# Filling TensorE's planned waits in the opening with products of constants in any free PSUM bank (chunk-selected attention and a squared-ReLU layer, one core)

## The chip, the cores and the metric

The kernel runs on one core of one Trainium2 chip. TensorE (PE; its weight loads PEld) multiplies into PSUM, VectorE (DVE) and ScalarE (ACT) read PSUM and compute, GpSimd (POOL) computes and issues loads, SyncE (SP) issues stores and transposing DMAs. Times are device microseconds of one execution; the metric is the median over executions. The granted clock is the share of TensorE's full clock that was passed to it.

## The reference, cut to what matters

Inputs are q, k, v of 4 batches, 8 heads, 768 tokens, 64 dims, and two weights of 512 x 2048 and 2048 x 512, all f32.

```python
k_min, k_max = min and max of k over chunks of 32 tokens      # 24 chunks
ub     = sum_d maximum(q * k_min, q * k_max)                  # an upper bound of the scores per chunk
ub     = where(causal by chunk, ub, -1e9)
top    = the 6 chunks of largest ub, for each query
scores = where(chunk in top and causal, q k^T / 8, -1e9)
attn   = exp(scores - max) / (sum + 1e-9)
x      = (attn @ v), heads side by side                       # 3072 x 512
out    = relu(x @ w_in)^2 @ w_out                             # 3072 x 512
```

## The kernel before, in words

Tokens go in tiles of 128, six to a batch. In the first tile of a batch no chunk has to be chosen (a query sees at most 4), so the four first tiles have a path of their own. They are loaded with two tokens to a partition: batches 0 and 1 of k and q by SP as f32 (`raw`, L427), then converted to bf16 by DVE or ACT; batches 2 and 3 by GpSimd. `first_transposes` (L582) turns them with 16 transposes of 64 x 64 for each of k and q of a batch. `first_attention` then presets two PSUM banks with a causal mask (`preset`, L614: two products of 512 columns), adds the scores (L623, eight products), exponentiates on ACT (L639), multiplies with v (L630) and divides on DVE (`normalise`, L652 and L654). `turn_back` (L298, the helper `transpose`) brings the first keys back to token order (`kb`).

All other tiles go through pairs of heads. `stage_a` prepares one pair: transposes of keys and queries (`kT`, `qT`, L298), minimum and maximum of each chunk (`kr`, L753, DVE), the positive and negative parts of the queries (`qp`, `qm`, L769, DVE), bounds (`ub`, L703 and L705), the six best (`ubm` L778, `m` L711, `selb` L783, all DVE), the selection turned (`sT`) and copied beside the keys and queries (`kqc`, L292 on DVE, L290 on ACT). `stage_b` computes scores with the selection folded in (L839), exponentials (L861), causal masks (L816 and L819) and products with v (L850). `ffn` turns x (`xt`), multiplies by `w_in` (`up`, L923), applies ReLU and the square (L930, L932, L942), and multiplies by `w_out` (`down`, L955).

The order of all this is fixed ahead by a planner, the class `Plan`. Each operation has a due time, costs on the engines that may run it, the operations that it needs and the tiles that it uses. `order` keeps a time for each engine and for each PSUM bank (`tp` has 1, `ps` 3, `av` 2, `ff` 2), and picks what can start first; `write` then emits the operations in that order. Semaphore waits are put in from the data. The planner counts a TensorE operation double while its start lies before `WARM` (8.0 planned us).

The planner also fills TensorE's waits with work whose result nobody reads, so that TensorE isn't idle: the constant tile `warm` (all ones) is multiplied. This happens in two places. The operation `made["warm"]` opens TensorE's queue with 5 products of 512 columns. And in `order`, an operation that starts before `FILL` (26.0 planned us) and whose PSUM tiles are all new gets `fill` products, as many of 0.216 as fit in the time between TensorE's last operation, or the bank's release, and its start; they go into that operation's own new bank just ahead of it. Where the tile is bf16, four transposes of `warm` stand for each product. What comes of this rule in the program: four transposes of 128 x 128 ahead of batch 0's key transposes (`T`), and two products of 512 columns ahead of batch 3's presets.

Of the kernel before, what the change touches and what calls it, by code (L numbers as in the profile page):

```python
# [9 lines left out]
F32 = mybir.dt.float32  # L10
# [23 lines left out]
class Op:  # L34
    def __init__(self, where, due, fn, needs, tiles, packets, turns):
        self.where, self.due, self.fn, self.turns = where, due, fn, turns
        self.needs, self.tiles, self.packets = needs, tiles, packets
        self.engine = None
        self.start = self.end = None
        self.fill = 0  # L40


class Transfers:
# [37 lines left out]
class Plan:  # L81
# [8 lines left out]
    BUSY = 0.11  # L90
    SLOWER = {}
    WARM = 8.0
    FILL = 26.0
    NEVER = 1e9

    def __init__(self, slots, keep_warm, wait):
        self.wait = wait
        self.slots = slots
        self.keep_warm = keep_warm
        self.ops = []  # L100
        self.loads = []

# [14 lines left out]
    def order(self):  # L117
        free = {e: 0.7 for e in ("PE", "ACT", "DVE", "POOL", "SP")}
        slots = {tag: [(0.0, i) for i in range(n)] for tag, n in self.slots.items()}
        waiting = {}  # L120
        count = {}
        for op in self.ops:
            for t in op.tiles:
                t.left = len(t.users)
            count[op] = len(op.needs)
            for n in op.needs:
                waiting.setdefault(n, []).append(op)
        ready = [op for op in self.ops if not count[op]]
        landed, done = [], []
        port = {"DVE": 0.0, "POOL": 0.0}  # L130
        dma = Transfers()
        while ready:
            found = []
            for op in ready:
                if op.packets and not op.turns and op is not self.loads[len(landed)]:
                    continue
                at = 0.0
                new = {}
                for t in op.tiles:
                    if not t.held:  # L140
                        new[t.tag] = new.get(t.tag, 0) + 1
                for tag, n in new.items():
                    at = max(at, sorted(slots[tag])[n - 1][0]
                             if n <= len(slots[tag]) else self.NEVER)
                if at == self.NEVER:
                    continue
                if op.packets and not op.turns and len(landed) >= 8:
                    at = max(at, landed[-8].end)
                for engine, cost in op.where.items():
                    st = max(at, free[engine])  # L150
                    for n in op.needs:
                        same = n.engine == engine and not n.packets
                        lag = (0.0 if engine == "PE" else self.BUSY) if same                             else self.HAND_OVER[n.engine]
                        st = max(st, n.end + lag)
                    for t in op.tiles:
                        if t.psum:
                            for e, end in t.last.items():
                                if e != engine and "PE" not in (e, engine):
                                    st = max(st, end + self.HAND_OVER[e])
                    if op.port and engine in port:  # L160
                        st = max(st, port["DVE" if engine == "POOL" else "POOL"])
                    found.append((st, op, engine, cost))
            assert found, "nothing can start"
            first = min(found, key=lambda f: (f[0], f[1].number))
            st, op, engine, cost = min(
                (f for f in found if f[2] == first[2] and f[0] <= first[0] + self.wait),
                key=lambda f: (round(f[1].due, 6), f[0], f[1].number))
            ready.remove(op)
            if engine == "PE":
                op.fill = 0  # L170
                fresh = [t for t in op.tiles if t.psum]
                if st < self.FILL and fresh and not any(t.held for t in fresh):
                    room = max([free[engine]] + [min(slots[t.tag])[0] for t in fresh])
                    op.fill = max(0, int((st - room - 0.3) / 0.216))
                if st < self.WARM:
                    cost *= 2
            op.engine, op.start, op.end = engine, st, st + cost
            free[engine] = op.end
            if op.port and engine in port:
                port[engine] = op.end  # L180
            if op.packets:
                dma.add(op)
                if not op.turns:
                    landed.append(op)
            for t in op.tiles:
                if not t.held:
                    t.held = True
                    slot = min(slots[t.tag])
                    slots[t.tag].remove(slot)
                    t.slot = slot[1]  # L190
                t.last[engine] = max(t.last.get(engine, 0.0), op.end)
                t.left -= 1
                if not t.left:
                    slots[t.tag].append(
                        (max(u.end + self.HAND_OVER[u.engine] for u in t.users),
                         t.slot))
            for n in waiting.get(op, ()):
                count[n] -= 1
                if not count[n]:
                    ready.append(n)  # L200
            done.append(op)
        assert len(done) == len(self.ops), "operations left"
        return sorted(done, key=lambda op: op.start)

    def write(self):
        for op in self.order():
            for t in op.tiles:
                if t.tile is None:
                    t.tile = t.make(t.slot)
            if op.fill:  # L210
                self.keep_warm([t for t in op.tiles if t.psum][0].tile, op.fill)
            op.fn(op.engine)


# [1 line left out]
def kernel(  # L216
# [9 lines left out]
    nc = tc.nc  # L226
# [44 lines left out]
    psav = ctx.enter_context(tc.tile_pool(name="psav", bufs=1, space=PSUM))  # L271
# [3 lines left out]
    plan = Plan({"tp": 1, "ps": 3, "av": 2, "ff": 2, "e": 6, "h2": NFI + 6, "ht": 3,  # L275
                 "ob": 3, "kt": 3, "nt": 6,
                 "vn": B - 1, "x": 2, "xT": 2,
                 "st": 2, "kr": 2, "qp": 2, "qm": 2, "ubm": 2, "m8": 2, "rc": 2}, lambda *a: keep_warm(*a), P["wait"])
    POOLS = {"tp": pst, "ps": pss, "av": psav, "ff": psf, "e": epool, "h2": hpool,
             "ht": hpool, "ob": opool, "vn": ld, "nt": ldt, "kt": tpool}  # L280
# [16 lines left out]
    def transpose(dst, src):  # L297
        nc.tensor.matmul(dst, lhsT=src, rhs=ident, is_transpose=True,  # L298
                         start=True, stop=True)
# [5 lines left out]
    warm = consts.tile([128, 128], BF16, tag="warm")  # L305
# [55 lines left out]
    made = {}  # L361
# [176 lines left out]
    t_first = {}  # L538
    x_done = {}

    def keep_warm(dst, n):

        size = 1
        for dim in dst.shape[1:]:
            size *= dim
        dst = dst if len(dst.shape) == 2 else dst.rearrange(
            {3: "p a b -> p (a b)", 4: "p a b c -> p (a b c)"}[len(dst.shape)])
        if dst.dtype == F32:
            size = min(size, 512) // 128 * 128 or size
            for _ in range(n * 512 // size):  # L550
                nc.tensor.matmul(
                    dst[:, 0:size].rearrange("p (a b) -> p a b", b=min(size, 128)),
                    lhsT=warm, rhs=warm[:, 0:min(size, 128)].unsqueeze(1).to_broadcast(
                        [128, size // min(size, 128), min(size, 128)]),
                    start=True, stop=True)
        else:
            for _ in range(4 * n):
                transpose(dst[:, 0:128], warm)

    def warm_up(n):  # L560
        keep_warm(psav.tile([128, 4, 128], F32, tag="av.0", name="wt"), n)

    made["warm"] = plan.op({"PE": 1.08}, -999, lambda _: warm_up(5), [made["ones"]])

    class Turned:
        def __init__(self, b):
# [416 lines left out]
    for what in P["later"].split():  # L983
        nm, b = what[0], int(what[1])
        at = 20 * NP * b - 70 + 5 * "kqv".index(nm)
# [21 lines left out]
    for b in range(B):  # L1007
        x = buffer("x", [128, NS, d_model])
        x_done[b, 1] = []
        for p in range(NP * b, NP * (b + 1)):  # L1010
# [4 lines left out]
            x, lambda t, b=b: x_done[b, 1], [S * b + 128 * t for t in range(1, NT)],  # L1015
# [48 lines left out]
```

## Time and profile before

| what | us |
|---|---|
| median of 3 executions | 266.44 (265.9 to 266.63) |
| the profiled execution | 266.1 |
| its span, first to last instruction | 264.4 |
| TensorE busy in it | 253.8 |
| VectorE, ScalarE, GpSimd busy | 175.2, 187.0, 128.9 |
| mean granted clock of TensorE | 0.981 |

The rows below come from that one execution. In the rows of a timeline the first number is the start and the second the time from the first start to the last end of the group; `[1.92 <-X]` is idle time of the engine ahead of it, and what ended it. Products are pipelined on TensorE: the duration of one has a tail that lies beside the next.

### The profile page before, as it was taken

To read this page: it belongs to the slowest core of one execution; us is meant where nothing else is said; L and a number is where in the kernel's file an instruction comes from. 1 tells how busy PE (TensorE), PEld (TensorE's weight loads), DVE (VectorE), ACT (ScalarE), POOL (GpSimd) and SP (SyncE) were. 2 spreads that over 40 slices of the span, in tenths; PEclk is the share of its full clock that TensorE was granted. 3 is DMA by queue.
4 is the path that set the end of the run, shared out by engine and by line. 5 is a ranking of instruction groups with operands and counts; after the bars stand their busy time and mean duration, and the time that the engine had idled before them with its cause. 6 is when DMAs were issued, how large, how long until landed. Compare 5 with 4: busy or idle time off the path is not lost.

```text
span 264.4 us, 6715 instructions
## 1 busy us (share of the span) xinstructions
PE 253.8 (96%) x2479; PEld 164.4 (62%) x2479; DVE 175.2 (66%) x637; ACT 187.0 (71%) x377; POOL 128.9 (49%) x197
## 2 busy tenths in 40 slices
PE   6498999999999999999999999999999999999995
PEld 2375855666587666666678654667876544765443
DVE  6479999988799986986676993567876400455000
ACT  6278978879579997989978972789896511677111
POOL 8897789699769999996210770112111100000000
PEclk9659999999999999999999999999999999999999
DMA  7999999999993995999999921443010052100122
GB/s 125 170 182 162 175 142 182 169 131 178 184 144 75 130 160 127 78 165 158 154 136 159 198 47 59 119 93 98 2 40 2 10 131 92 69 0 2 40 79 79
DMA packets 112960, 29.40 MB, mean 111 GB/s; under 512 B 103328, under 2 KB 109984, under 8 KB 112928
## 3 DMA queue, kind: packets, MB, share of 16 engines
q0 software_dynamic: 73040, 13.11, 64.3%
q1 hardware_dynamic: 39888, 15.87, 29.3%
q8 instruction: 19, 0.31, 0.5%
q14 instruction: 13, 0.11, 0.1%
HBM read 27.26 MB, written 6.29 MB: 127 GB/s over the span
## 4 chain that ended last, share of the span: by engine, by line
PE 80%; DMA 6%; DVE 5%; ACT 4%; issue 2%; SPq 1%; ACTq 0%; DVEq 0%
PE py L955 29%; PE ph L923 28%; PE ps L839 12%; PE av L850 6%; DMA sT<-selb 4%; DMA raw<-in_q_dram 3%; ACT e L861 2%; DVE kqc L292 1%; PE kT L298 1%; ACT ht L930 1%; PE T L582 1%; PE qT L298 1%; SPq L427 1%; DVE m L711 1%; PE ps L623 1%
## 5 line engine op out<-in xcount | busy, mean ns | idle before, releaser
L923 PE MATMUL ph<-xT,w_in_sb 128*128 128x256 bf16 (+2 forms) x592 | 95.6, 304 | 0.3 <-ACT ht L930 0.2
L955 PE MATMUL py<-w_out_sb,h 128*128 128x512 bf16 (+2 forms) x400 | 90.5, 370 | 0.0
L861 ACT ACTIVATE e<-ps 128x512 bf16<-128x512 f32 x160 | 86.4, 607 | 5.9 <-PE ps L839 3.0
L923 PEld LDWEIGHTS <-w_in_sb 128*128 128x128 bf16 x592 | 55.8, 97 | 23.8 <-issue 1.1
L930 ACT ACTIVATE ht<-ph 128x384 bf16<-128x384 f32 (+2 forms) x122 | 55.0, 454 | 17.2 <-PE ph L923 13.3
L955 PEld LDWEIGHTS <-h 128*128 128x128 bf16 x400 | 36.6, 97 | 35.1
L839 PE MATMUL ps<-kqc 88*128 88x128 bf16 (+1 forms) x320 | 52.9, 272 | 0.5 <-DVE kqc L292 0.2
L942 POOL TENSOR_TENSOR h<-ht 128x384 bf16<-128x384 bf16 (+2 forms) x50 | 38.5, 791 | 23.0 <-ACT ht L930 19.5
L942 DVE TENSOR_TENSOR h<-ht 128x256 bf16<-128x256 bf16 (+2 forms) x98 | 32.8, 338 | 14.9 <-ACT ht L930 11.2
L819 POOL TENSOR_SCALAR_AFFINE_SELECT e<-e 128x128 bf16<-128x128 bf16 (+1 forms) x54 | 17.3, 342 | 50.4 <-ACT e L861 50.4
L290 ACT COPY ob<-py 128x512 f32<-128x512 f32 (+2 forms) x23 | 13.1, 569 | 37.9 <-PE py L955 37.6
L850 PEld LDWEIGHTS <-e 128*128 128x128 bf16 x640 | 31.5, 97 | 8.5 <-POOL e L819 0.5
L839 PEld LDWEIGHTS <-kqc 88*128 88x128 bf16 x320 | 26.3, 97 | 12.3 <-issue 1.3
L850 PE MATMUL av<-vn,e 128*128 128x65 bf16 x480 | 32.3, 193 | 0.2
L816 DVE TENSOR_TENSOR e<-e,tri 128x128 bf16<-128x128 bf16 (+1 forms) x74 | 17.0, 239 | 16.7 <-ACT e L861 16.0
L932 DVE TENSOR_SCALAR ht<-ph 128x256 bf16<-128x256 f32 (+2 forms) x26 | 12.4, 477 | 18.2 <-PE ph L923 18.0
L654 DVE TENSOR_TENSOR x<-av,rc 128x320 bf16<-128x320 f32 (+1 forms) x40 | 18.7, 475 | 0.9
L753 DVE TENSOR_REDUCE kr<-kT 128x24 bf16<-128x768 bf16 x16 | 14.7, 947 | 1.5 <-PE kT L298 1.5
L711 DVE MAX8 m<-ubm 128x8 f32<-128x24 f32 x160 | 15.2, 168 | 0.2
L753 DVE TENSOR_REDUCE kr<-kqt 128x24 bf16<-128x768 bf16 x16 | 14.4, 944 | 1.0 <-DMA kqt<-nt 1.0
L850 PE MATMUL av<-v,e 128*128 128x65 bf16 x160 | 14.6, 193 | 0.0
L292 DVE COPY kqc<-sT 24x384 bf16<-24x384 bf16 (+1 forms) x36 | 10.6, 295 | 4.0 <-PE sT L298 1.8
(88 smaller groups left out, 247.3 us busy)
## 6 DMA issues: line engine op xcount, KB each, us to landing
out_dram<-ob SPq DMA_DIRECT2D x23, 256.0 KB, 2.2
kqc<-kqt SPq DMA_DIRECT2D x16, 176.0 KB, 3.7
w_in_sb<-in_moe_w_in_dram POOLq DMA_DIRECT2D x4, 512.0 KB, 7.4
w_out_sb<-in_moe_w_out_dram POOLq DMA_DIRECT2D x4, 512.0 KB, 9.5
vn<-in_v_dram POOLq DMA_DIRECT2D x15, 128.0 KB, 6.9
nt<-in_k_dram POOLq DMA_DIRECT2D x10, 128.0 KB, 9.4
nt<-in_q_dram POOLq DMA_DIRECT2D x10, 128.0 KB, 4.2
kqn<-in_k_dram POOLq DMA_DIRECT2D x8, 80.0 KB, 7.3
```

The costliest lines, as they stand in the source:

```text
L654: return plan.op({"DVE": 0.06 + 0.00108 * D * n}, due, lambda _: nc.vector.tensor_mul(x(), av[:, :, 0:D], rc[:, 0:n].unsqueeze(2).to_broad ...
L711: nc.vector.max(out=m8[:, i, hh], in_=ubm[:, i, hh])
L753: t0 + 5 + 2 * mm, lambda _, mm=mm, f=f: nc.vector.tensor_reduce(kr[:, mm].rearrange("d (t c) -> d t c", c=128 // CH) if b >= BY_DMA else ...
L816: nc.vector.tensor_mul(e, e, tri.unsqueeze(1).to_broadcast([128, n, 128]))
L819: nc.gpsimd.affine_select(out=e, in_=e, compare_op=ALU.is_ge, fill=0.0, base=0, channel_multiplier=-1, pattern=[[0, n], [1, 128]])
L839: nc.tensor.matmul(ps[:, 128 * c:128 * (c + nt)], lhsT=kqs[:, s, hh, 128 * j:128 * (j + 1)], rhs=kqs[:, s, hh, S + 128 * (t0 - 1):S + 128 ...
L850: nc.tensor.matmul(av[:, t - 1], lhsT=e[:, 128 * c:128 * (c + 1)], rhs=value_tile(b, h, j), start=(i == 0 and c == 0), stop=(i == len(BANK ...
L861: nc.scalar.activation(e.tile, ps.tile, ACT.Exp, scale=scale), [sc], [ps, e])
L923: nc.tensor.matmul(ph.tile, lhsT=w_in_sb[:, ki, 128 * f:128 * (f + 1)], rhs=xT[:, c0 // 128:c1 // 128, ki], start=(ki == 0), stop=(ki == N ...
L930: nc.scalar.activation(ht.tile, ph.tile, ACT.Relu)
L942: at[0] + P["h2"], lambda e: vector(e).tensor_mul(h2[f][:, c0:c1], ht.tile, ht.tile), [op], [ht, h2[f]], port=True)))
L955: nc.tensor.matmul(py.tile, lhsT=h2[f][:, 128 * t:128 * (t + 1)], rhs=w_out_sb[:, f, c0:c1], start=(f == 0), stop=(f == NFI - 1))
```

## The change

The planned order and the planned times stay as they are; what is emitted between TensorE's operations is new. `order` no longer computes `fill`; it records when each PSUM tile is taken and given up (`since`, `until`, and `banks`, the tiles of each bank). `write` looks at the gap ahead of every TensorE operation that starts before 30 planned us. It asks `spare` for the PSUM bank that has been free the longest at that moment, whichever pool it belongs to, takes the gap from TensorE's last operation (or the bank's release plus 0.1) to the start, and if that is 0.2 or more it emits `keep_warm` into that bank: one product of 256 columns for each 0.1092 of the gap less 0.08. No transposes are used as filling any more.

In the program built from it, 40 filling products of 256 columns stand at eleven places, where there were four transposes and two products of 512 columns at two places:

| products | ahead of | waits of the first one, beside the bank's earlier products |
|---|---|---|
| 4 | `T`, keys of batch 0 (L582) | |
| 7 | `T`, keys of batch 1 | |
| 2 | `T`, queries of batch 0 | |
| 4 | scores of batch 0 (L623) | |
| 2 | presets of batch 2 (L614) | ACT's copy of batch 2's keys |
| 6 | the first turn of x (`xt`) | ACT's first exponential of batch 2 |
| 4 | `T`, queries of batch 3 | ACT's exponential of batch 1 |
| 6 | presets of batch 3 | |
| 3 | the first scores of pair 0 (L839) | |
| 1 | query transposes of pair 1 (`qT`) | |
| 1 | the first `up` product (L923) | |

Four of TensorE's later operations take over a bank from a filling and wait for its end: the presets of batch 2, the bounds `ub` of pair 0, the `qT` of pair 1 and the first `up`; a turn of x and some fillings wait for the end of an older one. The opening ten products of 256 columns replace five of 512. All other instructions of all engines are the same, in the same order.

```diff
-    FILL = 26.0
+    FILL = 30.0
+    LEAST, SPARED, EARLY = 0.2, 0.08, 0.1
...
-            if engine == "PE":
-                op.fill = 0
-                fresh = [t for t in op.tiles if t.psum]
-                if st < self.FILL and fresh and not any(t.held for t in fresh):
-                    room = max([free[engine]] + [min(slots[t.tag])[0] for t in fresh])
-                    op.fill = max(0, int((st - room - 0.3) / 0.216))
-                if st < self.WARM:
-                    cost *= 2
+            if engine == "PE" and st < self.WARM:
+                cost *= 2
...
+                    if t.psum:
+                        t.since = slot[0], st
+                        self.banks.setdefault((t.tag, t.slot), []).append(t)
...
+    def spare(self, at):
+        found = []
+        for (tag, slot), held in self.banks.items():
+            found.append((max([0.0] + [t.until for t in held if t.since[1] < at]),
+                          tag, slot))
+        return min(found)
+
     def write(self):
+        idle = 0.0
         for op in self.order():
+            if op.engine == "PE":
+                free, *bank = self.spare(op.start - 1e-6)
+                room = op.start - max(idle, free + self.EARLY)
+                if idle and op.start < self.FILL and room >= self.LEAST:
+                    self.keep_warm(bank, int((room - self.SPARED) / 0.1092))
+                idle = op.end
...
-            if op.fill:
-                self.keep_warm([t for t in op.tiles if t.psum][0].tile, op.fill)
             op.fn(op.engine)
...
-    def warm_up(n):
-        keep_warm(psav.tile([128, 4, 128], F32, tag="av.0", name="wt"), n)
-
-    made["warm"] = plan.op({"PE": 1.08}, -999, lambda _: warm_up(5), [made["ones"]])
+    def keep_warm(bank, n):
+        tag, slot = bank
+        dst = POOLS[tag].tile([128, 2, 128], F32, tag=f"{tag}.{slot}", name="wt")
+        for _ in range(n):
+            nc.tensor.matmul(dst, lhsT=warm,
+                             rhs=warm.unsqueeze(1).to_broadcast([128, 2, 128]),
+                             start=True, stop=True)
+
+    made["warm"] = plan.op({"PE": 1.08}, -999, lambda _: keep_warm(("av", 0), 10), [made["ones"]])
```

More of the change, by code (lines that the diff above doesn't have):

```diff
@@ L39, in __init__ @@
         self.start = self.end = None
-        self.fill = 0
 class Transfers:
@@ L99, in __init__ @@
         self.keep_warm = keep_warm
+        self.banks = {}
         self.ops = []
@@ L193, in order @@
                 if not t.left:
-                    slots[t.tag].append(
-                        (max(u.end + self.HAND_OVER[u.engine] for u in t.users),
-                         t.slot))
+                    t.until = max(u.end + self.HAND_OVER[u.engine] for u in t.users)
+                    slots[t.tag].append((t.until, t.slot))
             for n in waiting.get(op, ()):
```

17 lines of the change are left out of this document (removed).

## The prediction

> **What bounds the kernel now.** I read the page first, then the list of TensorE's waits, then the table of stretches of time, then the chain of waits and the instructions in order of time. The page: span, busy time, and two of its 40-slice rows.
>
> ```profile
> span 264.4 us, 6715 instructions
> PE 253.8 (96%) x2479; PEld 164.4 (62%) x2479; DVE 175.2 (66%) x637; ACT 187.0 (71%) x377; POOL 128.9 (49%) x197
> ...
> PE   6498999999999999999999999999999999999995
> ...
> PEclk9659999999999999999999999999999999999999
> ```
>
> TensorE is the bound: 253.8 of 264.4 us. Its idle time is in the first four slices (6.6 us each) and in the last; the granted clock is low in slices two and three alone. TensorE's own waits, the longest and one small one:
>
> ```profile
> PE T L582 <- DVE f L292: 3.3, 2, 1.9
> ...
> PE T L582 <- DVE kf L292: 0.8, 1, 0.8
> ...
> PE xt L298 <- ACT e L639: 0.2, 1, 0.2
> ```
>
> The two conversions of raw tokens to bf16 cost TensorE 3.3 us; no load stands in that list, so TensorE is never behind a transfer that it waits for directly. Next the table of stretches (us of the stretch, then busy us of PE, PEld, DVE, ACT and POOL, then granted clock). Two rows of 0.1 us find the edges of the low clock: 0.91 in 8.70 to 8.80 and 0.90 in 19.00 to 19.10 put the drop at 8.78 and the return at 19.02. That is 10.24 us, and I cut the opening into stretches of a third of it, 3.41 us.
>
> ```profile
> 8.70:8.80 0.10, 0.10 (x7) 0.10 (x8) 0.00 (x0) 0.00 (x0) 0.03 (x1) 0.91 2.33 156
> 19.00:19.10 0.10, 0.10 (x4) 0.10 (x2) 0.10 (x2) 0.10 (x2) 0.10 (x1) 0.90 1.28 242
> ```
>
> ```profile
> 1.96:5.37 3.41, 3.41 (x12) 1.41 (x10) 2.91 (x19) 3.25 (x5) 3.41 (x5) 1.00 0.96 176
> 5.37:8.78 3.41, 0.70 (x25) 0.43 (x25) 1.96 (x3) 0.00 (x0) 3.36 (x4) 1.00 1.53 193
> 8.78:12.19 3.41, 1.73 (x38) 1.36 (x39) 1.39 (x2) 0.85 (x2) 2.38 (x3) 0.50 2.32 157
> 12.19:15.61 3.42, 3.42 (x71) 2.81 (x71) 2.08 (x3) 2.48 (x5) 3.42 (x6) 0.50 2.40 161
> 15.61:19.02 3.41, 3.25 (x30) 2.05 (x31) 2.27 (x8) 2.45 (x5) 3.41 (x5) 0.50 1.53 187
> 19.02:22.43 3.41, 3.02 (x66) 1.90 (x63) 3.37 (x19) 2.35 (x6) 1.67 (x3) 1.00 2.22 169
> 22.43:25.85 3.42, 2.96 (x40) 2.12 (x41) 3.27 (x13) 3.23 (x7) 3.42 (x5) 1.00 1.58 164
> ...
> 33.00:66.00 33.00, 32.93 (x344) 20.37 (x342) 29.93 (x101) 27.65 (x53) 29.52 (x40) 1.00 1.60 160
> ```
>
> The clock fell after a stretch with 0.70 us of TensorE work. It did not come back after a stretch that was full (12.19 to 15.61), but after the next, hardly fuller one. What differs is the kind of work. The same table for transposes alone, first those of the helper at L298, then those of the first tiles at L582:
>
> ```profile
> 12.19:15.61 3.42, 0.82 (x6) 0.56 (x6) 0.50 2.40 161
> 15.61:19.02 3.41, 1.38 (x12) 1.23 (x13) 0.50 1.53 187
> ...
> 22.43:25.85 3.42, 1.40 (x16) 0.99 (x16) 1.00 1.58 164
> ```
>
> ```profile
> 5.37:8.78 3.41, 0.54 (x23) 0.43 (x25) 1.00 1.53 193
> ...
> 12.19:15.61 3.42, 1.70 (x48) 1.43 (x48) 0.50 2.40 161
> ```
>
> Without transposes the full stretch has 3.42 - 0.82 - 1.70 = 0.90 us of work (clock stays low), the next 3.25 - 1.38 = 1.87 (clock rises), and 22.43 to 25.85 has 2.96 - 1.40 = 1.56 and keeps the high clock. I read it so: products count, transposes hardly do, and less is needed to keep the clock than to win it. The Trainium skill, "TensorE: Matmul & The Clock Gate", Part 4 (PE-mode transpose), says that a transpose does not count as busy time in the same way; the trace agrees (3.42 us busy at 0.50).
>
> The chain of waits through the low clock (start, us, what), and rows that price the same work at the two clocks:
>
> ```profile
> 10.71 0.66 PE T L582 x11
> ...
> 12.13 0.61 PE ps L623 x8
> 12.74 0.75 PE kT L298 x6
> 13.50 0.99 PE T L582 x19
> ...
> 18.08 0.55 PE qT L298 x5
> ...
> 42.47 0.42 PE kT L298 x6
> ...
> 47.46 0.86 PE py L955 x4
> ```
>
> ```profile
> 1.13 2.31 PE L551 MATMUL wt<-warm 128*128 128x512 bf16 x5 [1.13 <-DVE warm L362]
> ...
> 10.71 0.64 PE L582 MATMUL T<-ident,f 64*64 64x64 bf16 x16 [1.43 <-DVE f L292]
> 11.27 0.61 PE L298 MATMUL kb<-ident,kf 128*128 128x128 bf16 x4
> ...
> 19.93 0.44 PE L582 MATMUL T<-ident,f 64*64 64x64 bf16 x16
> ...
> 21.93 0.40 PE L623 MATMUL ps<-t,kf 64*128 64x128 bf16 x8
> ...
> 26.90 0.27 PE L923 MATMUL ph<-xT,w_in_sb 128*128 128x256 bf16 x1
> ```
>
> ```profile
> 13.53 0.96 DVE L753 TENSOR_REDUCE kr<-kT 128x24 bf16<-128x768 bf16 x1 [1.46 <-PE kT L298]
> ...
> 18.65 0.49 DVE L769 TENSOR_SCALAR qp<-qT 128x640 bf16<-128x640 bf16 x1 [1.08 <-PE qT L298]
> ...
> 23.08 1.35 DVE L292 COPY kqc<-sT 24x384 bf16<-24x384 bf16 x4
> ```
>
> **The change, part by part.** A filling product has 256 columns. Four of 512 take 0.86 at the high clock, so one of 256 takes 0.11; five of 512 in 2.31 at the low clock give about 0.21. The opening's 10 x 256 in place of 5 x 512 is the same work: nothing. Engines other than TensorE keep instructions and order, so no load or store is moved past a queue.
>
> *Fills before 12.13 (4, 7, 2, 4 products).* The first four replace four transposes in the wait that ends at 7.45, and take some 0.65 there. The seven (0.75) lie between the transposes at 7.45 and those at 8.68, under the 0.8 that these wait for DVE's copy. The two lie in the wait up to 10.71. The four (0.43) sit ahead of the scores at 12.13, which wait for a DVE copy of 0.70 that starts when the transposes end. Cost nothing at the high clock; cover gone: at the low clock the last four take 0.85, the `kb` transposes ahead of them (11.27, four products of half the fill's columns, so 0.43 of issue) let them in at 11.70, and the scores go from 12.13 to 12.55.
>
> *What they do to the clock.* In 5.37 to 8.78 there would be 0.97 us of products (two of the first four, 0.21, and the seven) where there were none, in 8.78 to 12.19 0.87 (six fills and the start of the scores, 0.23). The bounds are 0 (fell) and 1.56 (kept). Both values are nearer to 1.56, so I take it that the clock holds.
>
> *What the high clock is worth.* The conversion that ends at 10.65 waits for a transfer and does not move. From there: 16 transposes 0.44 for 0.64, scores 0.40 for 0.61, key transposes 0.42 for 0.75. So DVE's first reduction starts 0.20 + 0.21 + 0.33 = 0.74 earlier, at 12.79. DVE then works through to the idle 1.08 ahead of 18.65. TensorE's work from 13.50 to 18.63, 5.13 us, takes 0.56 (key transposes) to 0.69 (L582) of that at the high clock: at least 1.6 saved, so the queries' transposes end by 18.63 - 0.74 - 1.6 = 16.3, with the two fills ahead of the presets (0.22, and a tail of 0.27 - 0.11 = 0.16 that the presets wait for) by 16.7. DVE wants them at 18.65 - 0.74 - 1.08 = 16.83: all the idle goes, and the step is 1.82 earlier. What is late next is DVE itself, busy 3.37 of 3.41 us up to 22.43; it cannot go faster, so 1.82 is the most.
>
> *Fills after 16.8 (6, 4, 6, 3, 1, 1).* Six ahead of the first turn of x (0.65) lie under DVE's pass over the queries. Four (0.43) and six (0.65, for two of 512 before, 0.43) delay the last first-tile scores by up to 0.65; the selection's transposes behind them wait for DVE, so I cost them at nothing (bounds 0 and 0.65). The three (0.32) end as DVE's copies at 23.08 release the scores: nothing. The last two cost 0.11 each, with little cover in a stretch at 2.96 of 3.42: 0.2.
>
> *Sum.* -1.82 + 0.2 = -1.6 us at 27 us. From 33 on TensorE is busy 32.93 of 33.00 and waits for no load, so the shift reaches the end: 266.1 - 1.6 = 264.5 for the profiled execution. The median shown, 266.44, lies 0.34 above that, which gives 264.8. Bounds for this case: -0.9 (the fills' 0.65 is paid) to -2.0 (the last two are hidden).
>
> **The rivals.** *R1, the clock falls at 8.78 all the same and returns at 19.02.* For it: nothing shows that 0.97 is enough, and 0.90 did not win the clock. Against it: 0.90 was a test of winning, not of keeping. Fills then cost double: 0.42 ahead of the scores at 12.55, and the two ahead of the presets 0.43 + 0.16 = 0.59, in a stretch without idle time. That is +1.0, 267.4. It decides as soon as the drop at 8.78 shows. The Trainium skill, same page, Part 1 ("A second HAM failure mode"), tells of short idles between groups of products that make the clock swing; no run here shows it, and by that rule R1 would hold.
> *R2, it falls at 8.78 but returns at 15.61*, since that stretch gains about 0.5 of products over the 0.90. DVE's reduction then starts at 13.53 + 0.42 and its idle can go: 0.42 - 1.08 + 0.2 = -0.4, 266.0.
> *R3, it holds one stretch and falls at 12.19*: the 0.74 is partly won, and the presets pay 0.59 or the later idle goes: between -0.7 and +0.5, 266.3 in the middle.
> The same page, Part 1, gives a window of 3413 ns and a return to half clock after an idle one; a stretch with 0.97 us of products is not idle, so by that rule the forecast holds. The trace's 10.24 us is three such windows.
>
> **How the numbers follow.** Forecast 0.52, R1 0.26, R2 0.11, R3 0.11. A measurement tells about 0.3% (0.8 us) from no change. Faster: nearly all of the forecast and a little of R2 and R3, 0.51. Slower: R1 less the part that lands under +0.8, and collisions that I have not priced, 0.25. Same: 0.24. The forecast's own range is 264.3 to 265.6; the range that leaves out 2 in 10 reaches over R2 and R3 to R1: 264.2 to 267.5.
>
> **What would show it.** Right: granted clock 1.00 in all slices from the second on; the transposes at 10.71 in 0.44; DVE's idle before the first `qp` gone and `qp` at 16.8; the first selection copy near 21.3 for 23.08; the same 1.6 us at 60 and at 200 us. Wrong: clock 0.50 after 8.78, scores at 12.5, presets that start after 16.5; or fills at 19 to 21 that push the selection's transposes behind DVE. If TensorE shows a wait for a load after 30 us, the pass-through fails.

## The result and the profile after

| | before | after |
|---|---|---|
| median of 4 executions each, us | 266.46 (265.9 to 266.63) | 269.0 (268.41 to 269.63) |
| ratio, with its 95% interval | | 1.010 (1.0071 to 1.0128) |
| profiled execution, and its span, us | 266.1, 264.4 | 268.82, 265.9 |

The changed kernel is slower by 1.0%, where 264.8 us and a gain had been forecast. The profiled execution after has 2.9 us outside its span, where that of before has 1.7, and the three other executions of after have spans of 266.7 to 267.9; so the spans of this pair of traces (+1.5) understate the loss, and a second trace of the same kernel is used beside it below.

The page of after: the slices of TensorE and of its granted clock.

```profile
PE   7699999999999999999999999999999999999995
...
PEclk9759999999999999999999999999999999999999
```

TensorE's first four slices (6.6 us each) went from 6, 4, 9, 8 to 7, 6, 9, 9: its waits are filled in part. But slices two and three of the clock are still low. The table of stretches, cut where this trace's clock changes (columns as before: busy PE, PEld, DVE, ACT, POOL, then the granted clock):

```profile
3.27:6.68 3.41, 2.73 (x9) 0.99 (x7) 2.44 (x9) 1.99 (x3) 3.41 (x5) 1.00 1.43 205
6.68:10.09 3.41, 2.00 (x41) 1.37 (x41) 0.89 (x2) 0.59 (x1) 3.28 (x4) 1.00 1.91 181
10.09:13.51 3.42, 2.61 (x34) 1.82 (x35) 1.39 (x2) 0.59 (x2) 2.93 (x4) 0.50 2.36 155
13.51:16.92 3.41, 3.37 (x64) 2.62 (x64) 2.63 (x4) 2.69 (x5) 3.41 (x5) 0.50 2.05 172
16.92:20.33 3.41, 3.40 (x30) 2.24 (x30) 1.66 (x7) 1.86 (x5) 2.65 (x4) 0.50 1.57 195
20.33:23.75 3.42, 3.42 (x71) 2.75 (x69) 3.38 (x18) 2.49 (x5) 2.46 (x3) 1.00 2.29 148
```

The low stretch is 10.24 us long as before, only moved: 10.09 to 20.33 for 8.78 to 19.02. It follows a stretch with 2.00 us of TensorE work. The same table for the filling products alone (tile `wt`):

```profile
6.68:10.09 3.41, 1.33 (x9) 1.00 1.91 181
```

These are nine products, as many as the prediction counted as 0.97 us in a stretch (1.33 with their tails). They are not the same nine: the stretches lie elsewhere in this execution, so the seven and the two that follow them fall into one, and the first four (4.94) into the one before. They did not hold the clock. TensorE in order of time, up to the first `up` product; the presets of the trace before stand below it:

```profile
4.94 1.06 PE L556 MATMUL wt<-warm 128*128 128x256 bf16 x4
...
10.90 0.64 PE L579 MATMUL T<-ident,f 64*64 64x64 bf16 x16 [1.96 <-DVE f L302]
...
11.87 1.06 PE L556 MATMUL wt<-warm 128*128 128x256 bf16 x4
12.86 0.61 PE L620 MATMUL ps<-t,kf 64*128 64x128 bf16 x8
...
16.27 0.61 PE L556 MATMUL wt<-warm 128*128 128x256 bf16 x2
16.93 1.01 PE L611 MATMUL ps<-ahead,ident 128*128 128x512 bf16 x2
...
28.82 0.38 PE L920 MATMUL ph<-xT,w_in_sb 128*128 128x256 bf16 x2
```

```profile
15.54 1.03 PE L614 MATMUL ps<-ahead,ident 128*128 128x512 bf16 x2
```

And the chain that ended last, over the same time (start, us, what):

```profile
12.07 0.85 PE wt L556 x4
12.93 0.54 PE ps L620 x7
...
16.33 0.56 PE wt L556 x2
...
16.93 1.01 PE ps L611 x2
...
22.87 0.76 PE wt L556 x6
```

The fillings are now links of the chain. Against before, where the conversion let the transposes start at 10.71, everything from 10.90 is 0.19 late by the load of the raw queries. The scores start at 12.86 for 12.13 (0.73 late, so 0.54 from the four fillings), the presets at 16.93 for 15.54 (1.39 late, 0.66 more), and the first `up` at 28.82 for 26.90 (1.92 late). So the opening costs 1.7 us by itself.

The list of TensorE's waits after has no load in it:

```profile
PE T L579 <- DVE f L302: 2.9, 2, 2.0
PE wt L556 <- DVE warm L372: 1.1, 1, 1.1
```

### The profile page after: what moved, and what is told of

Same layout as the page of the kernel before. It is cut to its first block, busy times and chain, and to the rows that moved or that the text cites. A ratio compares the mean times of both kernels' runs of the same rounds, so it can differ in the third digit from the quotient of the medians.

```text
span 265.9 us, 6768 instructions
## 1 busy us (share of the span) xinstructions
PE 256.3 (96%) x2493; PEld 167.7 (63%) x2518; DVE 176.2 (66%) x637; ACT 187.1 (70%) x377; POOL 129.5 (49%) x197
## 4 chain that ended last, share of the span: by engine, by line
PE 76%; DMA 9%; DVE 6%; POOL 3%; ACT 2%; SPq 1%; issue 1%; ACTq 0%; DVEq 0%; POOLq 0%
PE py L952 27%; PE ph L920 24%; PE ps L836 10%; PE av L847 6%; DMA sT<-selb 3%; DMA raw<-in_q_dram 3%; DMA kqt<-nt 2%; DVE kqc L302 2%; DVE kr L750 2%; POOL vn L478 2%; PE wt L556 1%; DMA kqc<-kqt 1%; ACT e L858 1%; PE kT L308 1%; PE T L579 1%
## 5 line engine op out<-in xcount | busy, mean ns | idle before, releaser
L952 PE MATMUL py<-w_out_sb,h 128*128 128x512 bf16 (+2 forms) x375 | 86.6, 370 | 1.4
L478 POOL DMA_DIRECT2D vn<-in_v_dram x15 | 13.2, 911 | 0.0
```

The costliest lines, as they stand in the source:

```text
L478: load((nm, b), lambda _: nc.gpsimd.dma_start(out=nat[nm, b].tile[:, block(nm, j - 1), :, 0:D], in_=SRC[nm][b, :, 128 * j:128 * (j + 1)].r ...
L952: nc.tensor.matmul(py.tile, lhsT=h2[f][:, 128 * t:128 * (t + 1)], rhs=w_out_sb[:, f, c0:c1], start=(f == 0), stop=(f == NFI - 1))
```

## The experiments

All are the changed kernel with the planned order as it is. In most of them the number of filling products at each of the eleven places is written down in a list (after has 4, 7, 2, 4, 2, 6, 4, 6, 3, 1, 1); e8, e12 and e15 have no list and fill as after does. The edit that brings in the list is shown once, then the lists, and what else an edit changes beside them.

To compare two traces I take the start of the same TensorE instruction in both and subtract. This table, worked out from the timelines, gives that lag to the profiled execution before, in us (minus is earlier), near 10 us (how late the raw queries are converted: by their load, and in e3 and e7 also by a conversion of 1.10 for 0.69), 28, 110 and 160 us of the trace before; from 160 to the end it no longer changes. The last column is 160 less 110.

| kernel | 10 | 28 | 110 | 160 | 110 to 160 |
|---|---|---|---|---|---|
| after | 0.19 | 1.93 | 1.93 | 1.58 | -0.35 |
| after, second trace (e12) | 0.06 | 1.50 | 1.50 | 2.46 | +0.96 |
| e1, no fillings | 0.72 | 0.72 | 0.72 | 0.67 | -0.05 |
| e2, first three places | 0.30 | 0.30 | 0.28 | 1.92 | +1.64 |
| e3, last eight places | 0.81 | 0.63 | 0.62 | -0.02 | -0.64 |
| e4, clock held | 0.00 | -0.82 | -0.83 | 0.36 | +1.19 |
| e5, held, hidden places only | 0.86 | -1.05 | -1.04 | 0.45 | +1.49 |
| e11, a delay alone | 0.20 | 2.03 | 2.02 | 2.09 | +0.07 |
| e13, one product at each place | 0.66 | 1.40 | 1.40 | 2.41 | +1.01 |
| e6, no fillings, loads left out | 0.45 | 0.44 | 0.34 | -0.31 | -0.65 |
| e7, e5 with loads left out | 1.14 | -0.76 | -0.89 | -1.51 | -0.62 |
| e8, after with loads left out | 0.25 | 0.16 | 0.04 | -0.61 | -0.65 |
| e9, e5 with loads late | 0.33 | -1.56 | -1.72 | -2.35 | -0.63 |
| e10, no fillings, loads late | 0.59 | 0.59 | 0.58 | -0.06 | -0.64 |
| e14, e2 with loads late | 0.52 | 0.13 | 0.11 | -0.54 | -0.65 |
| e15, after with loads late | 0.53 | 2.33 | 2.33 | 1.68 | -0.65 |

### Which fillings cost

```diff
+        self.COUNTS = list(self.COUNTS)
...
-                    self.keep_warm(bank, int((room - self.SPARED) / 0.1092))
+                    n = self.COUNTS.pop(0) if self.COUNTS else 0
+                    if n:
+                        self.keep_warm(bank, n)
```

```diff
e1_no_fills
+    COUNTS = [0, 0, 0, 0, 0, 0, 0, 0, 0, 0, 0]
e2_first_three
+    COUNTS = [4, 7, 2, 0, 0, 0, 0, 0, 0, 0, 0]
e3_last_eight
+    COUNTS = [0, 0, 0, 4, 2, 6, 4, 6, 3, 1, 1]
e4_clock_held
+    COUNTS = [16, 7, 13, 4, 2, 6, 4, 6, 3, 1, 1]
```

> All eleven fillings are taken out (the opening ten products stay), and so are the four transposes and two products of the kernel before. Theory A (the clock is low from about 9 to 19 us whatever the fillings did, and each filling's own length is what the changed kernel pays): the clock still falls near 9 to 10 us and returns about 10.24 us later, and the time is that of the kernel before, 266.3 +- 0.5. Theory B (the fillings pay by the hand-over of their banks, the semaphore waits between a filling and the next operation): also 266.3, no difference here. Theory C (the loss is the place of the low clock in time, which differs from execution to execution and not because of the fillings): 266.5 to 269, as the changed kernel.

> Only the first three places are filled (4, 7, 2 products), which lie in waits for DVE copies and for a load. A: they are hidden and too few to hold the clock; low clock as in the changed kernel, time of the kernel before, 266.3 +- 0.5. B: the same, 266.3. A rival of A, that the transposes of batch 1 and the conversion are pushed back by these fillings: +0.5 or more, 267.

> Only the last eight places are filled (4, 2, 6, 4, 6, 3, 1, 1 products). A: all of the loss is here, 268.7 to 269.2: about +0.5 at the scores of batch 0, +0.6 at the presets of batch 2, and the rest between 19 and 29 us. If the first three places bear a part of the loss, 267.5 or less.

> Places 1 and 3, which are waits of 1.5 to 2.4 us on the chip, get 16 and 13 products for 4 and 2; the other places as in the changed kernel. If products in the low stretch were only too few to hold the clock: granted clock 1.00 from about 6 us on, first `qp` at about 17 us, 264.9 (-1.6 against the kernel before). If the clock falls all the same: the 16 and 13 products at the low clock push batch 0's transposes back, 269.5 or more. By theory B the clock may hold and the time still be above 266.5.

| kernel | median, us | against before at 266.12 |
|---|---|---|
| e1_no_fills | 266.48 | 1.0001 (0.9985 to 1.0017) |
| e2_first_three | 267.47 | 1.0047 (1.0018 to 1.0075) |
| e3_last_eight | 267.49 | 1.0045 (1.0019 to 1.007) |
| e4_clock_held | 266.66 | 1.0008 (0.999 to 1.0027) |

The fillings of before were worth nothing: without any the time is the same, though in e1's trace the clock was low for 13.65 us and not 10.24. The loss does not sit in the later eight places alone, as one expectation had it with 268.7 to 269.2; that was a miss. In e3's trace place 4 cost its 0.53 (0.81 to 1.34), but the clock was low for 6.83 us only and the opening ended 0.18 better than it was at 10 us. That trace is of the fastest of ten executions (266.07, with the median at 267.49), so it doesn't show where the others lost their time. e2 costs 0.5% too, and yet its opening adds nothing to its late load (0.30 at 10 and at 28): all that it lost in its trace it lost between 110 and 160 us. And e4, where 16 and 13 products hold the clock, is 2.03 us early at 18 us, 0.82 early at 28 and 110, and 0.36 late at the end: the 264.9 expected for a held clock is a miss, and the 266.5 or more of theory B fits in number only, since the trace puts 1.2 us on the later fillings and 1.2 on 110 to 160 us. So there are two questions: what the opening loses, and what happens at 110 to 160 us.

### The clock held, and the values of batch 3 left out

e5 holds the clock in its trace and fills only where TensorE waits long. The other three test the transfers at 115 to 150 us: ahead of them, from 113.8 to 117.3 us, GpSimd issues the loads of five blocks of v of batch 3, of which the first is used at 174 us. In these three kernels those five loads are left out, with one memset of that tile, and the values of batch 2 stand in their place, so batch 3's output is another.

```diff
e5_held_hidden
+    COUNTS = [16, 7, 13, 4, 0, 8, 2, 0, 0, 0, 0]
e6_no_v3 (no fillings), e7_held_no_v3 (as e5), e8_after_no_v3 (as after)
+            if b == 3:
+                return
...
-        load((nm, b), lambda _: nc.gpsimd.dma_start(
+        load((nm, b), lambda _: None if (nm, b) == ("v", 3) else nc.gpsimd.dma_start(
...
-        t = vfirst[:, b] if j == 0 else nat["v", b][:, j - 1]
+        t = vfirst[:, b] if j == 0 else nat["v", min(b, 2)][:, j - 1]
```

> Fillings only where the chip waits anyway, and enough of them to hold the clock: 16, 7, 13, 4, 0, 8, 2 products at places 1 to 7, none after. The opening should be 1.5 to 2 us earlier at 27 us than in the kernel before. Theory D (between 115 and 150 us transposing DMAs, not TensorE, set the pace, so that an earlier arrival is given back there and a later one is added to): 266.0 +- 0.6, TensorE ahead by 1.5 or more at 110 us and by less than 0.5 at 150. Rival E (the gain of the clock is real and passes through; the run before lost it to its later fillings): 264.6 +- 0.5, still ahead by 1.5 at 150.

> No fillings, and the five loads of batch 3's values after its first tile are left out (batch 2's values stand in for them, so batch 3's output is another); the order of all other work is the same. The five loads lie among the transposing DMAs of 113 to 130 us. D: these DMAs land 1 to 4 us earlier around 120 to 145, and the time is 265.5 to 266.4 or a little less, since without fillings TensorE waits little there. E: no change, 266.5.

> The fillings of the first kernel of this group, with the five loads left out as in the second. D: with the transfers out of the way the opening's gain reaches the end: 1.2 to 1.8 below the second kernel, 264.3 +- 0.6. E: the same distance as between the first kernel and the one without fillings and with all loads.

> The changed kernel with the five loads left out. If the opening alone bears its loss: above the second kernel of this group by what the opening loses, 1.3 to 1.9 (267.5 +- 0.5). If a part of the loss comes from the transfers (D, which add to a late arrival): the distance to the second kernel is 0.5 or more smaller than the 2.5 between the changed kernel and the one without fillings.

| kernel | median, us | against before at 266.39 |
|---|---|---|
| e5_held_hidden | 267.16 | 1.0023 (1.0004 to 1.0042) |
| e6_no_v3 | 265.81 | 0.9982 (0.9971 to 0.9993) |
| e7_held_no_v3 | 264.19 | 0.9929 (0.990 to 0.9957) |
| e8_after_no_v3 | 266.96 | 1.0025 (0.9999 to 1.0051) |

Holding the clock gains nothing with the loads (e5 is not faster than e1) and 0.53% without them (e7 against e6: 1.4 us of 266, and 1.6 by the medians). e5 came out above the 265.4 to 266.6 that theory D expected. A part of that is the clock: six of its ten executions show a mean granted clock of 0.992 to 0.994 and took 267.11 to 267.81, the four at 0.998 or more 265.82 to 266.51. In the traces a mean of 0.981 goes with 10.24 us at half clock and 0.987 with 6.83, so 0.994 is, by this estimate, one stretch of about 3.4 us, at a place that no trace shows. The four without it are still not 1.6 us faster than before. e8 spreads from 265.47 to 268.94 in the same way, the four at 0.987 and 0.994 below 266.5 and the six at 0.974 to 0.981 above 266.9; its trace has only 6.83 us at half clock and loses nothing in the opening.

The cause of what e5 gives back shows on ACT. Its instructions in order of time, the copies of the turned selection, which a transposing DMA of SP brings (`sT`), first before, then e5, then after's second trace:

```profile
129.14 0.51 ACT L290 COPY kqc<-sT 24x384 bf16<-24x384 bf16 x1 [0.22 <-DMA sT<-selb]
...
147.12 0.51 ACT L290 COPY kqc<-sT 24x384 bf16<-24x384 bf16 x1 [0.28 <-DMA sT<-selb]
```

```profile
129.85 0.51 ACT L304 COPY kqc<-sT 24x384 bf16<-24x384 bf16 x1 [2.17 <-DMA sT<-selb]
```

```profile
130.60 0.51 ACT L300 COPY kqc<-sT 24x384 bf16<-24x384 bf16 x1 [0.39 <-DMA sT<-selb]
...
149.58 0.51 ACT L300 COPY kqc<-sT 24x384 bf16<-24x384 bf16 x1 [1.27 <-DMA sT<-selb]
```

In e5 all engines come to this point a microsecond early and the DMA does not: it lands where it did before, or later. ACT stands 2.17 us in front of that copy with the next exponential queued behind it, and TensorE then waits for the exponential. The chain of e5 at this place, and TensorE's list of waits from 100 to 155 us:

```profile
119.28 10.54 DMA sT<-selb
...
130.87 0.60 ACT e L862
131.52 0.38 PE ps L840 x2
```

```profile
PE ps L840 <- ACT e L862: 1.8, 1, 1.8
```

In the trace before ACT and TensorE reached the same DMA nearly in step with it (0.22 and 0.28 of waiting). That is where the gain of the opening is given back. With the loads late (e9, next section) the same copy comes at 127.04, and ACT doesn't wait for it:

```profile
127.04 0.51 ACT L310 COPY kqc<-sT 24x384 bf16<-24x384 bf16 x1
```

### The same loads, all done, but later

Nothing is left out here. The five loads are issued by GpSimd after its 176th operation, near 156 us, and all else keeps its order.

```diff
+        self.later = []
...
+            pool += op.engine == "POOL"
+            if pool == 176:
+                while self.later:
+                    self.later.pop(0)(None)
...
-        load((nm, b), lambda _: nc.gpsimd.dma_start(
+        def go(_):
+            nc.gpsimd.dma_start(
...
+        load((nm, b), (lambda e: plan.later.append(go)) if (nm, b) == ("v", 3) else go,
```

```diff
e9_held_late_v3
+    COUNTS = [16, 7, 13, 4, 0, 8, 2, 0, 0, 0, 0]
e10_none_late_v3
+    COUNTS = [0, 0, 0, 0, 0, 0, 0, 0, 0, 0, 0]
e14_first_three_late_v3
+    COUNTS = [4, 7, 2, 0, 0, 0, 0, 0, 0, 0, 0]
e15_after_late_v3 (no list, fills as after)
```

> The held opening (16, 7, 13, 4, 0, 8, 2 products), and GpSimd issues the five loads of batch 3's values, first used near 174 us, after its last square near 156 us and not at 113 to 118 us. Everything is computed. D: the transposing DMAs of 115 to 150 us are freed as without these loads, and the opening's gain reaches the end: 264.4 +- 0.6, below the kernel before by 1.4 to 2.4. E, or if the loads come late for batch 3: 266.4 or more.

> No fillings, the five loads late as in the first kernel of this group. D: 265.8 +- 0.5, as without these loads, and 1.2 to 1.8 above the first kernel. E: no difference to the first kernel.

> The first three places alone (4, 7, 2), with the loads of batch 3's values issued after GpSimd's last square near 156 us. The same fillings with the loads in their old place gave 1.0047 of the kernel before. If that loss arises among the transfers of 115 to 150 us: 265.8 +- 0.3, as without fillings and with late loads. If it arises in the opening: 266.6 to 267.2.

> The changed kernel's fillings, with the loads of batch 3's values late. If the opening's part of the loss is 1.3 to 1.9 and passes as it is once the transfers are out of the way: 265.76 plus that, 267.0 to 267.7. If nothing but the transfers cost: 265.8.

| kernel | median, us | against before (266.27 for the first two, 266.1) |
|---|---|---|
| e9_held_late_v3 | 263.94 | 0.9909 (0.9892 to 0.9926) |
| e10_none_late_v3 | 265.76 | 0.9979 (0.9968 to 0.999) |
| e14_first_three_late_v3 | 265.68 | 0.9981 (0.9962 to 0.9999) |
| e15_after_late_v3 | 267.38 | 1.0027 (0.9992 to 1.0063) |

e9 beats both kernels, by 2.3 us against before. The three that differ in fillings now differ by what their openings do: e9 is 1.8 us below e10, e15 1.6 above it (1.3 by the two ratios, since each goes by its own runs of before), e14 equal to it. e15's median hides a spread from 265.50 to 268.85: its three fastest, 265.50 to 265.68 and so no slower than e10, have mean clocks of 0.986 to 0.994; of the five at 267.89 or more four have 0.974 to 0.981, and the traced one reads 1.00 (for that see the last section). e10 spans 265.47 to 266.01 over clocks of 0.967 to 1.00. By these figures the fillings cost most where the clock fell for long and next to nothing where it fell briefly, which compares executions and is no test. The changed kernel's own eight executions (after and e12) have 0.975 to 0.981, and one 0.999. The table of lags says the same more sharply: with the five loads late or left out the change from 110 to 160 us is -0.62 to -0.65 in all seven traces, whatever the lag at 110 (-1.72 to 2.33); with them in place it is anything from -0.64 to +1.64. The 0.5% of e2 are gone in e14, so they arose there and not in the opening.

What those loads do to the others shows in the view of one tile's DMAs. Five loads of k (`nt`) issued by GpSimd from 116 to 126 us, in us from issue to landing (least, median, most), with the idle time of GpSimd ahead of them; before, then e9:

```profile
its engine sat idle before it (us, times) until:
  DMA vn<-in_v_dram: 1.8, 2
...
DMA to landing us min/median/max: 12.5/17.1/18.1
```

```profile
its engine sat idle before it (us, times) until:
  issue: 0.2, 1
...
DMA to landing us min/median/max: 5.0/6.2/8.1
```

And the transposing DMAs of `sT` issued from 115 to 152 us, before, e5 and e9:

```profile
DMA to landing us min/median/max: 3.9/6.7/9.6
```

```profile
DMA to landing us min/median/max: 3.3/6.9/10.5
```

```profile
DMA to landing us min/median/max: 3.0/4.8/6.6
```

Five loads that nobody needs for 50 us slow the k loads nearly threefold, hold up their issue, and lengthen the DMA that ACT waits for. The Trainium skill, "DMA: Bandwidth & Descriptors", "Issuing engines are not separate DMA queues", says that DMAs from different engines run on the same 16 DMA engines and interleave; the traces agree: SP's transposes get shorter (9.6 to 6.6 us) when GpSimd's loads go. No run separates the two ways in which the five loads cost, sharing the transfers and holding up GpSimd's next issues.

### A late start alone, and one product at each place

e11 has no fillings, but 17 transposes of the constant tile ahead of batch 2's presets: a delay that is no product (the opening ten stay products). e13 has one product at each of the eleven places. e12 is the changed kernel once more.

```diff
e11_delay_alone
+    COUNTS = [0, 0, 0, 0, 17, 0, 0, 0, 0, 0, 0]
...
-            nc.tensor.matmul(dst, lhsT=warm,
-                             rhs=warm.unsqueeze(1).to_broadcast([128, 2, 128]),
-                             start=True, stop=True)
+            transpose(dst[:, 0, 0:128], warm)
e13_one_each
+    COUNTS = [1, 1, 1, 1, 1, 1, 1, 1, 1, 1, 1]
```

> No fillings but one: 17 transposes of the constant, ahead of the presets of batch 2 (place 5), where TensorE has no idle time. At the low clock they take 17 x 0.107 = 1.8 us. They are a delay by itself: were they counted as work, the clock would return earlier. If a delay in the opening reaches the end as it is: 268.2 +- 0.4. If the transfers add to a late arrival: 268.8 to 269.5. If the middle of the kernel swallows a delay: 267 or less.

> The changed kernel unchanged, beside the other kernels of this group, for its time on the same chip and a second trace. From the first comparison 1.010 of the kernel before, 269.0 +- 0.6. If the place of the free-running clock window decides much, its executions spread over 2 us or more and the second trace shows another opening than the first (+1.9 us at 27 us).

> All eleven places keep their filling and so their bank and its semaphore waits, but with one product each. A (the length of the fillings is what is paid): the one ahead of the presets of batch 2 costs 0.21 and a tail, the rest is small; 0.3 to 0.7 in the opening, 266.6 to 267.2. B (the hand-over of the banks is paid): as the changed kernel, 268.5 to 269.

| kernel | median, us | against before (266.27 for the first two, 266.1) |
|---|---|---|
| e11_delay_alone | 268.9 | 1.010 (1.0067 to 1.0134) |
| e12_after_again | 268.82 | 1.0091 (1.0073 to 1.0108) |
| e13_one_each | 268.49 | 1.0078 (1.0051 to 1.0105) |

e11's transposes stand in its timeline as

```profile
15.73 2.00 PE L312 MATMUL wt<-ident,warm 128*128 128x128 bf16 x17
```

and its lag is 2.22 behind them, 2.03 at 110 and 2.09 at the end: this late opening passes in full, while the early ones of e4 and e5 did not. That trace was taken at 268.16; the six executions run from 267.25 to 270.22, and the median, 268.9, lies in the range expected if the transfers add to a late arrival, so the trace doesn't settle it for the others. e12 repeats the loss (268.82 for 269.0). Its opening costs 1.44 (1.50 less 0.06), and 110 to 160 us adds 0.96. There its chain reads:

```profile
116.14 9.45 DMA vn<-in_v_dram
...
126.18 18.42 DMA nt<-in_k_dram
...
146.58 2.98 DMA sT<-selb
```

The value loads hold up the last k load, which holds up what leads to the next `sT`; ACT's copy waits 1.27 for that (quoted above), and TensorE for ACT.

e13 is a miss in its total: nearly three quarters of the products are gone (11 for 40) and four fifths of the loss stay (by the ratios). Its 268.49 is the number that theory B gave for the hand-over of the banks, but its trace doesn't bear B out. In it 0.66 of the lag is the raw queries' load and 1.01 arises from 110 to 160 us; the fillings themselves cost 0.74 (1.40 less 0.66), of which the one ahead of the presets takes 0.43 and the last two 0.31, the others next to nothing. Their rows:

```profile
16.20 0.40 PE L560 MATMUL wt<-warm 128*128 128x256 bf16 x1
16.65 1.01 PE L615 MATMUL ps<-ahead,ident 128*128 128x512 bf16 x2
...
27.87 0.27 PE L560 MATMUL wt<-warm 128*128 128x256 bf16 x1
28.30 0.92 PE L924 MATMUL ph<-xT,w_in_sb 128*128 128x256 bf16 x7
```

The operation that takes over the filling's bank waits for the end of its tail: 0.40 and 0.27 for one product of which 0.21 and 0.11 are issue. The dearest filling is the first one at a place where TensorE has no wait.

## Why the prediction was wrong

**The step that failed first: "I take it that the clock holds".** It put 0.97 us of products in a stretch between 0 (fell) and 1.56 (kept) and chose by nearness. Measured, a stretch with as many products, 6.68 to 10.09, was followed by 0.50; so was the first stretch on record in e8 (nine products) and e12 (ten). The signs of being wrong that it named showed: clock 0.50, the scores at 12.86, the presets at 16.93. In e2's trace it fell after one with ten:

```profile
5.43:8.84 3.41, 1.29 (x10) 1.00 1.58 189
```

Other traces had enough, e14 for one stretch and e9 for good (as e4, e5 and e7); the filling products alone in each stretch, e14 first:

```profile
4.75:8.16 3.41, 1.47 (x11) 1.00 1.63 182
8.16:11.58 3.42, 0.46 (x3) 1.00 2.39 157
11.58:14.99 3.41, 0.00 (x0) 0.50 2.45 155
```

```profile
4.75:8.16 3.41, 2.24 (x19) 1.00 1.58 185
8.16:11.57 3.41, 2.20 (x19) 1.00 2.19 163
```

Nine and ten products fell and eleven held (e14's stretch has the end of the opening's presets beside them), but the cut moves: in after's trace the first four products (4.94) lie ahead of the cut at 6.68 and don't count with the seven, in e14's trace they lie behind the cut at 4.75. So the same counts give either, by where the cuts happen to lie, and by these traces 13 products in the first three places are at the edge of what is needed. The prediction took the place of the stretches from one execution, and chose by nearness between two far bounds; its chances (0.52 against 0.48 for the three rivals in which the clock falls) said as much, its time did not. The Trainium skill, "TensorE: Matmul & The Clock Gate", Part 1 ("What's actually happening"), has the clock halve after an idle window, of 3413 ns and free-running. That the windows lie differently in each execution the traces agree with (the cuts are at 6.68 and 4.75); that only an idle one halves the clock they do not bear out, since a window with 2.00 us of TensorE work did.

**What the held clock is worth was right.** In e4, e5 and e9, where it held, the lag falls by 2.03, 2.03 and 2.02 from 10 to 18 us (e5: 0.86 to -1.17), and by 1.91 and 1.89 to 28 us in e5 and e9; the prediction had 1.82. In e4 the first `qp` starts at 16.77, for the 16.8 forecast. e9 against e10 gives 1.8 in the median.

**R1, the low clock with doubled prices, is what happened, and its two prices were nearly right.** The scores: 0.42 predicted, 0.54 measured; the presets: 0.59, and 0.66. The four fillings took 0.85 on the chain as worked out; the 0.12 that are over lie between the last filling and the first score, and no run shows their cause. The later fillings were mis-sized, and R1's sum left them out: 0.2 in the forecast, 0.53 in after's trace (1.92 less 1.39), 0.63 in e15's (2.33 less 1.70 at 16 us), and at the held clock of e4, where they are the same, 1.2 (2.03 early at 18 us, 0.82 at 28). So a held clock alone would have left the forecast's opening at -0.8 and not at -1.6; e5 and e9, with fewer of them, kept 1.9. In after's trace the six ahead of batch 3's presets are on the chain (22.87, 0.76), which had been costed at nothing with 0.65 as the bound. Together the opening lost 1.4 to 1.8 us for R1's 1.0.

**The second step that failed: "From 33 on TensorE ... waits for no load, so the shift reaches the end".** TensorE's list of waits is no evidence for that. It waits for ACT, and ACT for the DMA: the rows `[0.22 <-DMA sT<-selb]` and `[0.28 <-DMA sT<-selb]` stood in the trace before, on ACT, and the prediction did not use them. They say that ACT and the transfers arrive there together; hence an early opening gives back 1.2 to 1.5 us (e4, e5), and the forecast would have failed at this place even with the clock held: e5 does all that the forecast wanted of the opening in its trace, and is not faster in the median; its fastest execution, 265.82, gains 0.6 us. The sign that the prediction named, a wait of TensorE for a load after 30 us, never showed for the same reason.

**The sum.** After against before is +2.5 us. e15 against e10, where the loads are out of the way, gives +1.6 in the medians and +1.3 by the ratios for the fillings. The rest, 0.9 to 1.2, is put down to 110 to 160 us: e12's trace shows 0.96 there, the first trace -0.35. So that part is argued from one trace and not shown.

**What stays open.** How much the clock needs: between ten and eleven products in a stretch by these traces, but with few cuts seen. What brings the clock back: the prediction read that 1.87 us of work without transposes does and 0.90 does not, but e1's trace goes against it. There a full stretch with 3.42 less 1.07 of transposes, 2.35, left the clock at 0.50, and the next one, with 3.25 less 2.48, 0.77, was followed by 1.00:

```profile
14.82:18.24 3.42, 3.42 (x59) 2.16 (x54) 3.36 (x9) 2.03 (x4) 3.42 (x6) 0.50 1.87 173
18.24:21.65 3.41, 3.25 (x62) 3.02 (x62) 2.28 (x8) 2.78 (x7) 2.06 (x4) 0.50 1.86 185
```

Why some late arrivals at 115 us lose another microsecond (e2, e12, e13) and others don't (after's first trace, e3, e11): the transfers differ from execution to execution, and no run fixed one of them. Why e3, e8 and e15 had executions with a short fall of the clock, and the changed kernel none on record in its eight. And the raw queries' load, which landed 0 to 0.9 us later in all other traces than in the one trace before; nothing in the change touches it.

## What to carry to other kernels

Before a shift is passed on to the end, ask of every engine in the stages that carry transfers, not of TensorE alone, what it waits for: here a few tenths of waiting for a DMA on ACT marked a stage as fast as its transfers, and time won ahead of it was lost there. Filling a wait pays only if the wait is there on the chip and the filling is enough to hold the clock wherever its windows lie; a filling ahead of an operation that doesn't wait, and takes over the filling's bank, cost its tail too, even as a single product. Loads that are needed 50 us later should not share a stage with transfers that are needed at once: moving five of them made the gain of 1.8 us from the held clock real and gave 0.5 to 0.6 by itself.

## What was unexpected of the hardware

The view of stretches shows a granted clock of 1.00 up to the first clock record of a trace, even where TensorE runs at half of it: in e13, whose first record comes at 20.09 us, the presets at 16.65 take 1.01 as in after at 0.50, and the stretch reads

```profile
14.60:18.00 3.40, 3.34 (x58) 1.00 1.69 180
```

so there the rows' durations tell the clock, and the number does not. A mean clock of 0.998 or more in a run's list can hide such an opening, as e13's own does.

The k loads of 128 KB took up to 18.1 us where 8.1 was the most without five more loads beside them, so here the landing time of a load of one size went by what was in flight beside it.
